# A two-layer attention and gated-product kernel: its orders, PSUM banks and strip places written out, up to six product steps inside a value burst

## The chip, the cores and the metric

The kernel runs on one core of one Trainium2 chip. The metric is the device time of one execution in microseconds (us); lower is better.

## The reference

Four stages run over one sequence of 2048 tokens of width 448. Stages 0 and 2 are the attention `A`, stages 1 and 3 the gated product `B`; each adds its result to `x`. The same weights serve both rounds.

```
x = A_x
x = x + A(layernorm(x), wqkv, wo)        # stage 0
x = x + B(layernorm(x), w_gate, w_up, w_down)   # stage 1
x = x + A(layernorm(x), wqkv, wo)        # stage 2
x = x + B(layernorm(x), w_gate, w_up, w_down)   # stage 3

A: q, k, v = x @ wqkv, 16 heads of 28; each token attends to itself and to the
   7 tokens 2, 4, ... 14 places before it; softmax; weighted sum of v; @ wo
B: (x @ w_gate) * (x @ w_up) @ w_down, inner width 1792
```

## The kernel before

**Tiles and stages.** Every stage is cut into chunks of 256 or 512 tokens (`ACH`, `BCH`), and the chunks of the four stages follow each other interleaved (`SEQ`), so that attention work of one round lies beside gate and up products of the next stage. `build` describes the whole kernel as some 1576 operations. Each one (`Op`) is a short run of instructions on one engine, with the operations it depends on and the PSUM banks it takes (`acquire`) and gives back (`release`). An operation is known by its number, which is the order in which `build` adds it and is the same in both kernels.

**What TensorE does.** There are four kinds of operations on it.
- Ordinary products (line L489): queries and keys (`xnTa,WQK`), values (`WV,xnTa`), the output projection (`wo_g,oT`), gate and up (`xnTb,WGU`), down (`WD,hT`). They are made of *steps*: a step is two instructions, one on the upper and one on the lower 64 rows of the array, which run side by side.
- Score bursts (L964): 64 small products of `qk`, for two blocks of 120 tokens.
- Value bursts (L1001): 64 small products (64 columns each) of `E_sb` and `v_sb`, again for two blocks; the first burst of a stage has 32. There are nine in each attention stage.
- Strips (L492): an ordinary step can also be written as eight instructions of 32 output columns each. In this form it uses the array in the same tiling as a value burst and can stand *inside* the burst. The operation whose steps are used so is called the host; what is left of it follows the burst in the ordinary form.

**What sets the order.** `ORD` lists, for each engine, the numbers of its operations in the order in which they are to run. An entry `526+393` on TensorE is burst 526 with host 393. `schedule` walks through these lists with a model of the times (`run_pe`, `ready_at`, the constants at the head of `Sched`). It uses the model to pick PSUM banks (`pick_banks`: the one free longest) and to decide in what order releases are seen. For an entry with a host it lays up to two steps (`MAXALT`, `WEAVE`) evenly into the burst: for 64 small products after the 21st and the 42nd. `emit` then writes the instructions of each engine in that order and puts the semaphore waits in front of an operation.

**Queues.** SyncE issues nearly all transfers, in one queue in the order of `ORD["sp"]`; an issue that waits for a semaphore holds up all behind it. At the start these are the tokens (`x_sb`), the four pieces of `wqkv` for queries and keys (`hT` is their staging place; two pieces go through ScalarE's queue), `WV`, `wo_g`, and then the 14 pieces of `WGU`. Each of the latter waits for the landing of the third transfer before it (`link`, `DEPTH`). Before the first product of queries and keys, eight casts (L664) bring the staged pieces into `WQK`; the first such product needs the halves of all four pieces.

Of the kernel before, what the change touches and what calls it, by code (L numbers as in the profile page):

```python
# [25 lines left out]
MAIN = "R64"  # L26
BURST = "C32"
WEAVE = 2
MAXALT = 2
# [18 lines left out]
NBK = 8  # L48
# [9 lines left out]
ORD = {  # L58
# [5 lines left out]
}  # L64
SEQ = "A00 A01 B10 A02 B11 A03 A04 B12 A20 B13 A21 B14 B30 A22 B31 A23 B32 B33 B34".split()

# [57 lines left out]
class Sched:  # L124
    ENGS = ("pe", "act", "dve", "pool", "sp")
    PE_LAT = 205.0
    LAT = 75.0
# [1110 lines left out]
```

## Time and profile before

| what | value |
|---|---|
| median of 3 runs | 387.16 us (386.94 to 387.19) |
| profiled execution: span from first to last instruction | 384.9 us |
| TensorE matrix products busy | 379.2 us, 6340 instructions |
| VectorE busy | 280.7 us |
| ScalarE busy | 194.2 us |
| GpSimd busy | 10.3 us |

The page gives the profiled execution as its span; the run times are about 2.3 us longer, and this lies outside the first and last instruction. In a timeline, a row starts at the given time and merges instructions of one form that follow each other; since products overlap in the array, a row's length reaches beyond the start of the next. The time a piece takes on the path is therefore read from start to start. In a table by stretch, (x32) after a busy time counts the instructions that are under way in that stretch.

### The profile page before, as it was taken

The numbers are of one execution on the slowest core, as the hardware profiler recorded it, in microseconds if no ns is written. First come the engines' busy times: TensorE is split into PE (matmuls) and PEld (weight loads), VectorE is DVE, ScalarE is ACT, GpSimd is POOL, SyncE is SP. The second block draws the span as 40 slices with busy tenths as digits, with TensorE's granted clock in tenths as the row PEclk, the third lists the DMA queues.
The fourth block names the chain that finished last, engine by engine and source line by source line (L and its number), as shares of the span: only waits on it lengthen the run. The fifth ranks groups of instructions, "written<-read, shape, count | busy, mean of one in ns | idle before, by whom it ended". The sixth has DMA issues, their size and how long they took to land.

```text
span 384.9 us, 14276 instructions
## 1 busy us (share of the span) xinstructions
PE 379.2 (99%) x6340; PEld 212.9 (55%) x6340; DVE 280.7 (73%) x605; ACT 194.2 (50%) x384; POOL 10.3 (3%) x41
## 2 busy tenths in 40 slices
PE   8999999999999999999999999999999999999997
PEld 4556577555554444444566677544555544445664
DVE  6977989889878678487887887764877796455333
ACT  5987885744753653154273535455365353134220
POOL 7110000000000000000000000000000000000000
PEclk9999999999999999999999999999999999999999
DMA  8887332501410012214003117120135014013003
GB/s 275 200 188 192 91 79 54 76 2 32 93 28 14 17 34 52 55 27 63 12 3 73 33 20 100 27 43 9 21 41 75 3 24 85 2 33 52 3 4 131
DMA packets 55105, 22.76 MB, mean 59 GB/s; under 512 B 46132, under 2 KB 54148, under 8 KB 55044
## 3 DMA queue, kind: packets, MB, share of 16 engines
q1 hardware_dynamic: 54612, 21.34, 27.1%
q8 instruction: 50, 0.82, 0.9%
q10 hardware_dynamic: 432, 0.52, 0.4%
q14 instruction: 11, 0.09, 0.1%
HBM read 8.54 MB, written 2.71 MB: 29 GB/s over the span
## 4 chain that ended last, share of the span: by engine, by line
PE 94%; DVE 3%; ACT 2%; issue 0%; DVEq 0%
PE ps L489 84%; PE ps L964 3%; PE ps L1001 2%; PE ps L655 2%; PE ps L1107 1%; PE ps L492 1%; ACT qk L852 1%; DVE xn_sb L748 1%; DVE O_sb L1012 1%; ACT E_sb L971 1%; PE ps L758 0%; DVE R_sb L1026 0%; DVE oT L1039 0%; DVE x_sb L1056 0%; ACT R_sb L1027 0%
## 5 line engine op out<-in xcount | busy, mean ns | idle before, releaser
L489 PE MATMUL ps<-xnTb,WGU 64*128 64x512 bf16 (+1 forms) x1938 | 176.7, 333 | 0.0
L489 PEld LDWEIGHTS ps<-xnTb,WGU 64*128 64x128 bf16 x1938 | 95.2, 94 | 71.1 <-issue 1.2
L1092 ACT ACTIVATE g_sb<-ps 128x512 bf16<-128x512 f32 (+1 forms) x140 | 69.5, 511 | 111.9 <-PE ps L489 105.3
L1095 DVE TENSOR_TENSOR hT<-g_sb,ps 128x512 bf16<-128x512 bf16 (+1 forms) x140 | 77.9, 574 | 37.9 <-ACT g_sb L1092 35.0
L489 PE MATMUL ps<-WD,hT 64*128 64x448 bf16 x820 | 84.4, 349 | 0.1
L489 PEld LDWEIGHTS ps<-WD,hT 64*128 64x128 bf16 x820 | 39.0, 94 | 34.5 <-issue 0.4
L1056 DVE TENSOR_TENSOR x_sb<-x_sb,ps 128x448 bf16<-128x448 bf16 x62 | 36.8, 614 | 23.5 <-PE ps L489 23.5
L489 PE MATMUL ps<-xnTa,WQK 64*128 64x512 bf16 (+1 forms) x504 | 52.1, 353 | 0.1
L727 DVE BATCH_NORM_STATS2 st<-x_sb 128x6 f32<-128x448 bf16 x64 | 38.3, 615 | 1.9 <-DMA x_sb<-in_A_x_dram 1.5
L748 DVE TENSOR_SCALAR xn_sb<-x_sb,mv,rstd 128x896 bf16<-128x896 bf16 (+1 forms) x64 | 35.5, 569 | 5.2 <-ACT rstd L732 5.1
L971 ACT ACTIVATE E_sb<-ps 128x1024 bf16<-128x1024 f32 (+1 forms) x36 | 33.8, 983 | 10.4 <-PE ps L964 9.7
L489 PEld LDWEIGHTS ps<-xnTa,WQK 64*128 64x128 bf16 x504 | 24.1, 94 | 22.7 <-POOL v_sb L628 0.5
L981 DVE TENSOR_TENSOR E_sb<-E_sb,MK 128x1024 bf16<-128x1024 bf16 (+2 forms) x40 | 23.5, 610 | 12.7 <-ACT E_sb L971 12.5
L852 ACT ACTIVATE qk<-ps 128x1024 bf16<-128x1024 f32 (+1 forms) x26 | 23.2, 907 | 14.4 <-PE ps L489 14.2
L489 PE MATMUL ps<-wo_g,oT 64*128 64x448 bf16 x252 | 28.7, 350 | 0.4 <-DVE oT L1039 0.2
L1039 DVE TENSOR_TENSOR oT<-O_sb,R_sb 128x480 bf16<-128x480 f32 (+3 forms) x36 | 22.0, 624 | 3.2 <-ACT R_sb L1028 3.2
L1027 ACT ACTIVATE R_sb<-R_sb 128x480 f32<-128x480 f32 (+1 forms) x34 | 20.1, 604 | 7.2 <-DVE R_sb L1026 6.9
L1026 DVE STREAM_SHUFFLE R_sb<-O_sb 128x480 f32<-128x480 f32 (+1 forms) x34 | 22.8, 694 | 0.0
L489 PE MATMUL ps<-WV,xnTa 64*128 64x336 bf16 (+3 forms) x244 | 22.6, 304 | 0.1
L730 ACT ACTIVATE lnv<-mv,eps_sb 128x2 f32<-128x2 f32 (+1 forms) x33 | 9.4, 293 | 26.4 <-DVE mv L729 26.4
L1028 ACT ACTIVATE R_sb<-R_sb 128x480 f32<-128x480 f32 (+1 forms) x34 | 19.7, 599 | 0.2
L489 PEld LDWEIGHTS ps<-wo_g,oT 64*128 64x128 bf16 x252 | 11.9, 94 | 11.5 <-PE ps L489 1.0
(55 smaller groups left out, 190.6 us busy)
## 6 DMA issues: line engine op xcount, KB each, us to landing
out_dram<-x_sb SPq DMA_DIRECT2D x15, 112.0 KB, 1.8
WGU<-in_B_w_gate_dram SPq DMA_DIRECT2D x7, 224.0 KB, 4.3
WGU<-in_B_w_up_dram SPq DMA_DIRECT2D x7, 224.0 KB, 4.2
x_sb<-in_A_x_dram SPq DMA_DIRECT2D x3, 448.0 KB, 5.8
WD<-in_B_w_down_dram SPq DMA_DIRECT2D x2, 448.0 KB, 3.6
WD<-in_B_w_down_dram SPq DMA_DIRECT2D x2, 336.0 KB, 4.5
vt<-qk SPq DMA_DIRECT2D x42, 16.0 KB
xnTb<-xn_sb SPq DMA_TRANSPOSE x32, 3.1
```

Of the source, the lines that this page charges most:

```text
L489: return lambda E: E.matmul(out(), lhs(), rhs(), start=start, stop=stop)
L727: sc.add("dve", one(lambda E, B=B: E.bn_stats(st6[:, B, :], x_sb[:, B, :]), ("bn", li, B)), 525.0, deps=[("x", li - 1, B)] + ([("xn", li - ...
L748: sc.add("dve", one(lambda E, B=B, dst=dst, src=src: E.tensor_scalar(dst, src, mv[:, B, 0:1], rstd[:, B:B + 1], ALU.subtract, ALU.mult), ( ...
L852: return E.activation(dst, src, ACT.Copy) if hasattr(E, "activation") else E.tensor_copy(dst, src)
L971: return E.activation(E_sb[:, slot, 2 * hp:2 * hp + 2, 0:w], ps[:, b0:b0 + 2, 0:w], ACT.Exp, scale=SCALE)
L981: return E.tensor_tensor(e, e, m, ALU.mult)
L1026: sc.add("dve", one(lambda E: E.stream_shuffle(R_sb[:, rs, 0:w], O_sb[:, os_, 0:w], [DH] * 32), ("Rs", li, qb)), dve_est(w) + 100.0, deps= ...
L1027: sc.add("act", one(lambda E: E.activation(R_sb[:, rs, 0:w], R_sb[:, rs, 0:w], ACT.Ln), ("Rl", li, qb)), act_est(w, False), deps=[("Rs", l ...
L1039: return E.tensor_tensor(oT[:, :, a % HALF:a % HALF + z - a], O[:, :, a - tok:z - tok], R_sb[:, rs, 0:w].rearrange("p (h n) -> p h n", h=4 ...
L1056: sc.add("dve", one(lambda E: E.tensor_tensor(x_sb[:, B, :], x_sb[:, B, :], ps[:, bk[w], 0:D], ALU.add), ("x", li, B)), dve_est(D), deps=[ ...
L1092: sc.add("act", one(lambda E, gs=gs, bk=bk: E.activation(g_sb[:, gs, 0:nt], ps[:, bk[0], 0:nt], ACT.Copy), ("G", li, j, fc)), act_est(nt), ...
L1095: sc.add("dve", one(lambda E, gs=gs, bk=bk, fc=fc: E.tensor_tensor(hT[:, fc, hs, 0:nt], g_sb[:, gs, 0:nt], ps[:, bk[1], 0:nt], ALU.mult), ...
```

## The change

Three things change together.

1. **Orders.** All five lists of `ORD` are new. No operation is added or removed. Some 40 evacuations and casts go to another engine; among them the three casts (L664) that ScalarE had go to GpSimd, which now does all eight. In SyncE's queue the first transfers are reordered, and four of the `WGU` pieces now stand behind writes of `vt` (columns of the values of late query chunks).
2. **Banks.** `schedule` no longer holds a model of the times. It reads the banks of each operation from a new list `BANK`, walks the lists once, and adds the waits for the former holder of a bank.
3. **Strip places.** `MAXALT` is 6, and an entry with a host gives the places of its steps: `253+349@24.40` lays one step after the 24th and one after the 40th small product. A number that occurs twice means two steps at that place. There are 14 entries with a host in both kernels. Before, they hold 27 steps, afterwards 46, that is 19 more steps in strips. TensorE has 6454 products instead of 6340.

The core of the diff, the lists cut to the entries with hosts and to the heads of two queues:

```
-WEAVE = 2
-MAXALT = 2
+MAXALT = 6
...
 "pe", entries with a host:
-526+393 402+583 547+444 597+587 618+660 761+684 774+681
-918+846 939+852 1127+1009 1148+1187 1301+1226 1322+1235 1343+1237
+253+349@24.40 526+393@24.32.40 547+444@16.16.32.40 597+482@24.40
+618+560@24.40 761+684@8.24 774+678@24.40 918+846@8.24.32.40.48
+939+855@24.40 1127+1009@8.23.32.32.40 1148+1193@24.32.40.40
+1301+1235@8.16.24.40.48.48 1322+1227@16.24.40.48 1343+1313@24.32.48
...
 "sp", first entries (0 1 6 7 8 11: x_sb; 4 5: staged pieces 1 and 3; 9 10: WV):
-0 1 4 5 6 7 8 9 10 11 12 13
+0 4 1 6 7 5 8 81 9 10 11 79 82 84 83 12 13
...
 "pool", first entries (62 to 69: the eight casts):
-18 43 23 20 24 27 19 34 63 62 28 64 68 69
+18 23 31 27 43 19 38 34 32 24 39 20 62 63 66 67 64 68 25 69 65
...
+BANK = "44:01 110:67 114:23 130:67 ... "
...
     def schedule(self):
+        banks = {}
+        for x in BANK.split():
+            i, got = x.split(":")
+            banks[int(i)] = [int(c) for c in got]
...
+            op.acquire.b = banks[op.idx]
+            for i, b in enumerate(op.acquire.b):
+                if holder[b] is not None:
+                    rel = freed[holder[b]]
+                    key = ("rel", rel.idx, b)
+                    self.ready[key] = (rel, len(rel.ins) - 1)
+                    op.deps.append(key)
+                holder[b] = (id(op.acquire), i)
...
-                            cut = [len(op.ins) * (i + 1) // (k + 1) for i in range(k)] + [len(op.ins)]
+                    cut = [int(c) for c in cuts.split(".")]
+                    seq, a = [], 0
+                    for i, z in enumerate(cut + [len(burst.ins)]):
+                        seq += [(burst, n) for n in range(a, z)]
+                        a = z
+                        if i < len(cut):
+                            seq += [(host, fn) for fn in host.alt[i]]
+                    seq += [(host, n) for n in range(2 * len(cut), len(host.ins))]
```

More of the change, by code (lines that the diff above doesn't have):

```diff
@@ L58 @@
 ORD = {
[5 rows of a table removed]
[5 rows of a table added]
 }
+BANK = "44:01 110:67 114:23 130:67 133:23 136:01 139:23 154:23 157:01 160:45 163:01 178:01 181:67 184:23 187:01 199:67 201:23 203:01 205:45 211:45 215:2345 220:23 228:67 230:23 232:01 234:45 240:67 244:23 248:0167 253:45 265:45 269:6701 274:67 286:45 300:67 303:01 306:05 309:41 312:06 315:23 318:47 321:15 324:64 327:75 330:17 333:60 336:26 339:16 342:54 348:67 350:23 352:23 354:45 367:67 371:67 376:6745 381:23 393:45 397:0123 402:23 414:67 438:03 441:23 444:26 447:01 450:21 453:67 456:52 459:67 462:72 465:34 468:16 471:05 474:10 477:34 480:32 486:67 492:45 494:01 496:23 498:01 511:45 516:67 521:0123 526:23 538:34 542:2301 547:45 559:01 563:45 565:01 567:45 569:01 582:01 587:67 592:6745 597:45 609:45 613:0167 618:45 630:01 654:13 657:32 660:04 663:15 666:67 669:40 672:23 675:67 678:12 681:45 684:23 687:60 690:17 693:23 696:62 702:34 728:23 730:45 732:01 734:67 747:23 751:01 756:6723 761:45 769:0167 774:45 786:46 810:76 813:15 816:20 819:17 822:26 825:67 828:23 831:12 834:40 837:75 840:46 843:45 846:75 849:64 852:35 858:16 884:23 886:01 888:45 890:67 903:23 908:01 913:2301 918:23 930:74 934:0167 939:67 951:23 965:40 968:70 971:72 974:42 977:31 980:10 983:35 986:32 989:54 992:72 995:53 998:63 1001:75 1004:24 1007:67 1023:53 1026:43 1029:67 1032:01 1035:43 1038:52 1041:01 1044:01 1047:67 1050:23 1053:23 1056:32 1059:50 1062:24 1065:46 1093:01 1095:67 1097:45 1099:01 1112:67 1117:01 1122:6745 1127:23 1139:23 1143:4501 1148:01 1160:23 1184:53 1187:30 1190:24 1193:72 1196:75 1199:01 1202:17 1205:34 1208:67 1211:45 1214:51 1217:20 1220:67 1223:46 1226:45 1234:32 1262:01 1264:45 1266:67 1268:01 1281:45 1286:01 1291:01 1296:2367 1301:67 1313:13 1317:4501 1322:01 1334:07 1338:6701 1343:45 1355:76 1379:36 1382:24 1385:27 1388:72 1391:05 1394:41 1397:36 1400:13 1403:52 1406:75 1409:41 1412:60 1415:07 1418:63 1421:20 1429:14 1457:53 1460:65 1463:41 1466:03 1469:57 1472:02 1475:02 1478:56 1481:41 1484:57 1487:20 1490:35 1493:05 1496:73 1499:62 1507:45 1525:17 1528:34 1531:16 1534:12 1537:37 1540:63 1543:01 1546:63 1549:01 1552:41 1555:60 1558:71 1561:01 1564:72 1567:7 1570:6 1573:3"
 SEQ = "A00 A01 B10 A02 B11 A03 A04 B12 A20 B13 A21 B14 B30 A22 B31 A23 B32 B33 B34".split()
@@ L108 @@
     __slots__ = ("engs", "ins", "est", "deps", "mode", "prio", "acquire", "release", "idx", "eng",
-                 "dma", "lat", "after", "start", "end", "seen", "selfd", "tmin", "rdy", "alt", "pos")
+                 "dma", "lat", "after", "seen", "selfd", "tmin", "alt")
     def __init__(self, **kw):
@@ L125 @@
     ENGS = ("pe", "act", "dve", "pool", "sp")
-    PE_LAT = 205.0
-    LAT = 75.0
-    SAME = 60.0
-    SELF_LAT = 180.0
-    TAIL = {"pe": 0.0, "act": 125.0, "dve": 85.0, "pool": 100.0, "sp": 0.0}
-    SWITCH = 102.0
-    FETCH = 4.17
-    QUEUE = 64
-    AHEAD = 32
-    HEAD = 64
-    REFILL = 256.0
-    LINE = 256
-    LINE_T = ((75000.0, 4300.0), (24000.0, 4900.0), (11000.0, 5600.0), (-1.0, 5000.0))
     def __init__(self):
@@ L142, in __init__ @@
         self.ready = {}
-        self.fed = [(self.HEAD, 0.0)]
-        self.lines = [0.0, 0.0]
-        self.npos = 0
-        self.met = {}
     def add(self, engs, ins, est, deps=(), prio=0.0, mode=None, acquire=None, release=(), dma=None, lat=0.0, after=None, selfd=(), tmin=None, alt=()):
@@ L162, in add @@
         return op
-    def finish_of(self, key):
-        op, n = self.ready[key]
-        if op.end is None:
-            return None
-        if op.dma is not None:
-            return max(o.end + o.lat for o in self.dgroup[(op.dma, op.mode)])
-        if n == len(op.ins) - 1:
-            return op.end
-        return op.start + (op.end - op.start) * (n + 1) / len(op.ins)
-    def ready_at(self, op, eng):
-        r = 0.0
-        for k in op.deps:
-            f = self.finish_of(k)
-            if f is None:
-                return None
-            src = self.ready[k][0]
-            if src.dma is not None:
-                lat = 60.0
-            elif src.eng == eng:
-                lat = (self.SELF_LAT if k in op.selfd else 0.0) if eng == "pe" else self.SAME + self.TAIL[eng]
-            else:
-                lat = self.PE_LAT if src.eng == "pe" else self.LAT + self.TAIL[src.eng]
-            r = max(r, f + lat)
-        if op.tmin is not None:
-            r = max(r, op.tmin)
-        if op.after is not None:
-            if op.after.end is None:
-                return None
-            r = max(r, op.after.end)
-        return r
@@ L196, in pick_banks @@
-    def pick_banks(self, req, now):
-        ok = [self.holder[b] is None and self.free_at[b] + self.LAT <= now + 1e-6 for b in range(NBK)]
-        if req.pair:
-            pairs = [p for p in range(NBK // 2) if ok[2 * p] and ok[2 * p + 1]]
-            if len(pairs) < req.n // 2:
-                return None
-            pairs.sort(key=lambda p: max(self.free_at[2 * p], self.free_at[2 * p + 1]))
-            got = []
-            for p in pairs[:req.n // 2]:
-                got += [2 * p, 2 * p + 1]
-            return got
-        cand = [b for b in range(NBK) if ok[b]]
-        if len(cand) < req.n:
-            return None
-        cand.sort(key=lambda b: (ok[b ^ 1], self.free_at[b]))
-        return cand[:req.n]
@@ L213, in banks_for @@
-    def banks_for(self, item, now):
-        held, ok = list(self.holder), True
-        for op in item:
-            if op.acquire is not None:
-                got = self.pick_banks(op.acquire, now)
-                if got is None:
-                    ok = False
-                    break
-                for b in got:
-                    self.holder[b] = op.acquire
-        self.holder = held
-        return ok
-    def fed_at(self, i, ahead):
-        i = max(0, i - ahead)
-        for (n0, t0), (n1, t1) in zip(self.fed[-2::-1], self.fed[:0:-1]):
-            if n0 <= i:
-                return t0 + (t1 - t0) * (i - n0) / max(1, n1 - n0)
-        return 0.0
@@ L235, in run_pe @@
-    def run_pe(self, now, n, stream):
-        n0 = self.fed[-1][0]
-        t = now
-        if self.fed[-1][1] < now:
-            self.fed.append((n0, now))
-        lead = min(self.QUEUE, (now - self.fed_at(n0, self.QUEUE)) / self.FETCH)
-        end = now + stream
-        if n > lead:
-            end = max(end, now + (n - lead) * self.FETCH + self.REFILL)
-        while len(self.lines) * self.LINE <= n0 + n + self.AHEAD:
-            k = len(self.lines)
-            i = (k - 1) * self.LINE
-            if i <= n0:
-                at = self.fed_at(i, self.AHEAD)
-            else:
-                at = max(now, now + (end - now) * (i - n0 - self.AHEAD) / n)
-            at = max(at, self.lines[-1])
-            self.lines.append(at + next(t for t0, t in self.LINE_T if at >= t0))
-        k = (n0 + n) // self.LINE
-        if k * self.LINE > n0:
-            due = now + (end - now) * (k * self.LINE - n0) / n
-            end += max(0.0, self.lines[k] - due)
-        self.fed.append((n0 + n, end))
-        del self.fed[:-48]
-        return end
@@ L262, in waits @@
-    def waits(self, got):
-        need = {}
-        for op in got:
-            for k in op.deps:
-                src, n = self.ready[k]
-                if src.dma is not None:
-                    need[(src.dma, src.mode)] = (1, 0)
-                elif src.eng != "pe" or k in op.selfd:
-                    need[src.eng] = max(need.get(src.eng, (0, 0)), (src.pos, n))
-        new = 0
-        for w, v in need.items():
-            if self.met.get(w, (0, 0)) < v:
-                self.met[w] = v
-                new += 1
-        return max(0, new - 1)
@@ new lines, in schedule, with take @@
+    def schedule(self):
+        banks = {}
+        for x in BANK.split():
+            i, got = x.split(":")
+            banks[int(i)] = [int(c) for c in got]
+        freed = {}
+        for op in self.ops:
+            for bk, i in op.release:
+                freed[(id(bk), i)] = op
+        order = {e: [] for e in self.ENGS}
+        holder = [None] * NBK
+        seen = set()
+        def take(op, e):
+            assert op.idx not in seen and e in op.engs, (op.idx, e)
+            seen.add(op.idx)
+            op.eng = e
+            if op.acquire is None:
+                return
+            op.acquire.b = banks[op.idx]
+            assert len(op.acquire.b) == op.acquire.n and not (op.acquire.pair and any(x ^ 1 not in op.acquire.b for x in op.acquire.b))
+            for i, b in enumerate(op.acquire.b):
[5 more added lines that the diff above has]
+                holder[b] = (id(op.acquire), i)
+        for e in self.ENGS:
+            for x in ORD[e].split():
+                ids, _, cuts = x.partition("@")
+                got = [self.ops[int(i)] for i in ids.split("+")]
+                for op in got:
+                    take(op, e)
+                seq = [(got[0], n) for n in range(len(got[0].ins))]
+                if len(got) > 1:
+                    burst, host = got
+                    cut = [int(c) for c in cuts.split(".")]
[6 more added lines that the diff above has]
+                    seq += [(host, n) for n in range(2 * len(cut), len(host.ins))]
+                order[e].append((got, seq))
+        assert len(seen) == len(self.ops)
@@ L408, in schedule @@
         self.order = order
-        self.total = max(op.end + op.lat for op in self.ops)
     def emit(self, nc, block, sems):
```

123 lines of the change are left out of this document (removed), and 10 rows, old and new, of the table ORD.

## The prediction

> **What bounds the kernel now.** I read the page's head first, then the chain that ended last, then the busy times by stretch, then timelines of TensorE where it was not plain streaming.
>
> ```profile
> span 384.9 us, 14276 instructions
> ...
> PE 379.2 (99%) x6340; PEld 212.9 (55%) x6340; DVE 280.7 (73%) x605; ACT 194.2 (50%) x384; POOL 10.3 (3%) x41
> ...
> PE 94%; DVE 3%; ACT 2%; issue 0%; DVEq 0%
> ```
>
> TensorE (PE) carries 94% of the chain that sets the end. The stretches tell where it does not:
>
> ```profile
> core 0: us, PE busy (x) PEld busy (x) DVE busy (x) ACT busy (x) POOL busy (x), PEclk, DMA share, GB/s
> 8.00:22.00 14.00, 13.27 (x301) 8.23 (x296) 13.26 (x43) 13.15 (x33) 4.38 (x20) 1.00 0.83 222
> 22.00:36.00 14.00, 13.77 (x286) 8.26 (x269) 11.30 (x26) 12.26 (x24) 0.12 (x1) 1.00 0.80 180
> 36.00:52.00 16.00, 15.59 (x440) 8.14 (x438) 13.30 (x28) 13.47 (x21) 0.00 (x0) 1.00 0.51 125
> 52.00:66.00 14.00, 13.94 (x356) 11.99 (x357) 13.26 (x31) 9.43 (x22) 0.00 (x0) 1.00 0.16 34
> 66.00:130.00 64.00, 63.71 (x1127) 34.08 (x1124) 50.97 (x113) 37.15 (x69) 0.00 (x0) 1.00 0.24 41
> 130.00:258.00 128.00, 127.94 (x2122) 72.80 (x2118) 99.63 (x210) 57.05 (x119) 0.00 (x0) 1.00 0.24 42
> ```
>
> From 8 to 52 us (the head) TensorE is idle for 0.73 + 0.23 + 0.41 = 1.37 us, and VectorE and ScalarE are nearly as full as it is (13.26 and 13.15 of 14 us at first). From 52 to 130 us it is idle for 0.35 us, and from there to 258 us for 0.06 us. The granted clock is 1.00 throughout. So better orders can win at most about 1.4 us in the head and 0.35 us behind it; after 130 us they can only lose. What else is to be had lies inside TensorE's busy time, in the value bursts.
>
> **The bursts.** Timelines of TensorE: a burst without a host, one with a host, and ten gate-and-up operations without a burst.
>
> ```profile
> 27.23 0.68 PE L1001 MATMUL ps<-E_sb,v_sb 64*32 64x64 bf16 x64
> 27.85 0.74 PE L489 MATMUL ps<-WV,xnTa 64*128 64x448 bf16 x6
> ...
> 141.64 0.27 PE L1001 MATMUL ps<-E_sb,v_sb 64*32 64x64 bf16 x21
> 141.73 0.40 PE L492 MATMUL ps<-xnTb,WGU 64*32 64x512 bf16 x8
> 141.96 0.26 PE L1001 MATMUL ps<-E_sb,v_sb 64*32 64x64 bf16 x21
> 142.04 0.52 PE L492 MATMUL ps<-xnTb,WGU 64*32 64x512 bf16 x8
> 142.26 0.39 PE L1001 MATMUL ps<-E_sb,v_sb 64*32 64x64 bf16 x22
> 142.58 1.90 PE L489 MATMUL ps<-xnTb,WGU 64*128 64x512 bf16 x16
> ...
> 307.04 15.27 PE L489 MATMUL ps<-xnTb,WGU 64*128 64x512 bf16 x140
> 322.14 0.92 PE L489 MATMUL ps<-wo_g,oT 64*128 64x448 bf16 x8
> ```
>
> An ordinary step of 512 columns costs (322.14 - 307.04) / 70 = 0.216 us. A burst alone costs 27.85 - 27.23 = 0.62 us. The woven one takes 142.58 - 141.64 = 0.94 us and does two steps on the way, so the burst itself costs 0.94 - 0.43 = 0.51 us. The laying-in is worth 0.11 us a burst as it stands. Why a burst alone is so slow shows when it is cut finer:
>
> ```profile
> 27.23:27.35 0.12, 0.12 (x32) 1.00 1.26 286
> 27.35:27.45 0.10, 0.10 (x32) 1.00 1.37 198
> 27.45:27.72 0.27, 0.27 (x58) 1.00 0.08 2
> ```
>
> The first 32 products enter within 0.12 us. Then for 0.10 us the same 32 are under way and none enters; the other 32 then need 0.27 us. I read this as a window of 32 products: product n + 32 enters when product n has left. The Trainium skill ("TensorE: Matmul & The Clock Gate", section "Architectural detail: the array is 16× 32×32, not 1× 128×128") gives TensorE a queue of 64 instructions; a weight load and a matmul for each product make 32 products, and the trace agrees (x32). By its rule that matmuls also end in order (same page, "The mechanism"), a strip that is still running keeps everything behind it in the window.
>
> If the window never bound, 64 products would enter in 2 x 0.12 = 0.24 us, and the way out (27.72 to 27.85) is 0.13 us: 0.37 us. So a burst that is woven already can gain between 0 and 0.51 - 0.37 = 0.14 us. In the woven burst above, the first set of strips lasts 0.40 us and the second 0.52 us: the second enters one by one, because with the cut at 21 and 42 its strips are the 51st to 58th products, and from the 54th on they wait for the first set (the 22nd to 29th) to leave. With the cut at 24 and 40, 24 products and 8 strips fill the window exactly, and the next 16 products and the second strips (33rd to 56th) wait only for the first 24 small products, which leave long before the first strips end. The second set then lasts 0.40 us again: a gain of 0.12 us, of which I take 0.10.
>
> Sum over the bursts: 13 entries woven before and after, one of them half as long, 12.5 x 0.10 = 1.25 us. Burst 253 is newly woven: 0.62 - 0.41 = 0.21 us. Burst 402 loses its host: 0.11 us lost. That makes -1.35 us, with bounds of 0 (no cut helps; 253 and 402 cancel) and -1.9 us (0.14 each, 253 at 0.25). The 19 further steps are work that is moved, not removed. Inside the burst a step takes 141.96 - 141.73 = 0.23 us instead of 0.216 us, so they cost between 0 and 19 x 0.014 = 0.27 us; I take 0.1. That a third to sixth step hides anything more I don't count: with two well-placed ones the burst is already near 0.4 us.
>
> **The start.** The first query and key product needs the casts of all four staged pieces.
>
> ```profile
> 1.71 0.91 SPq L579 DMA_DIRECT2D hT<-in_A_wqkv_dram  x2
> 2.66 1.50 SPq L579 DMA_DIRECT2D x_sb<-in_A_x_dram  x3
> ...
> 6.37 1.07 POOL L664 COPY WQK<-hT 128x448 bf16<-128x448 bf16 x2 [0.25 <-DMA hT<-in_A_wqkv_dram]
> ...
> 7.43 1.04 ACT L664 ACTIVATE WQK<-hT 128x448 bf16<-128x448 bf16 x2
> 7.64 0.39 PE L489 MATMUL ps<-xnTa,WQK 64*128 64x256 bf16 x4
> ...
> x_sb<-in_A_x_dram SPq DMA_DIRECT2D x3, 448.0 KB, 5.8
> ```
>
> The last staged piece, issued at about 2.2 us (the second of the two in the first row), lands just ahead of 6.37 us, 4.1 us later. In the new queue two token transfers (224 and 448 KB) stand in front of it, and it is issued two places, 0.9 us, later, at 3.1 us. If it takes 4.1 us again, it lands at 7.2 us; if it takes the 5.8 us of the big token transfers, at 8.9 us. I take 8.2, nearer to the latter, since those tokens now go first. With a cast of 0.53 us the product can start at about 8.8 instead of 7.64 us: 1.2 us late, with bounds of 0.1 and 1.8. The Trainium skill ("DMA: Bandwidth & Descriptors", "Queues, rings and completion order") says that each engine takes a queue's descriptors in ring order; by that rule the upper part of the range is right, without it the lower.
>
> This start need not reach the end. The tokens land earlier by what the piece lost, VectorE begins sooner, and ScalarE, which has no idle time to speak of, is rid of three casts (3 x 0.52 = 1.6 us), which GpSimd does in time it has. The first gate product ends the head:
>
> ```profile
> 50.01 1.93 PE L489 MATMUL ps<-wo_g,oT 64*128 64x448 bf16 x16 [0.24 <-DVE oT L1039]
> 51.92 0.83 PE L489 MATMUL ps<-xnTb,WGU 64*128 64x256 bf16 x12
> ```
>
> TensorE has 51.92 - 7.64 - 1.37 = 42.9 us of work up to there. From 8.8 us on without any idle time it would arrive at 51.7, 0.2 us sooner; with all the idle time left, 1.2 us later. The idle time was waiting for the engines that are now relieved, so I take +0.1 us.
>
> **The rest.** Of the 0.35 us between 52 and 130 us I take 0.1 as won. Behind it, some fifteen evacuations change between ScalarE and VectorE; TensorE hid them all (0.06 us idle in 128), VectorE has 28 us to spare there, and I cost them at nothing. If a few banks come free late, each costs what is left of an evacuation, up to 0.5 us in all.
>
> **Sum.** -1.35 + 0.1 + 0.1 - 0.1 = -1.25 us. The span of 384.9 becomes 383.6. The runs' median is 2.3 us above the span, which I leave unchanged: 387.16 - 1.25 = 385.9 us.
>
> **Rivals.** *The head opens up:* the late start is absorbed in full and the waits between 52 and 130 us go too, with the bursts at their bound: -1.9 - 0.2 - 0.35 = -2.45, 384.7 us. For it speaks that ScalarE is relieved; against it that TensorE's start is later.
>
> *The window is not what holds the bursts:* if the entry rate of 0.27 us for 32 products is set by something that strips use up too, the new cuts give nothing, the 19 steps cost 0.27 us, and with the head at +0.1: 387.5 us; with half of the gain 386.8. Against it: the first set of strips enters at full rate.
>
> *SyncE's queue makes the first gate product late, so the kernel is slower:* four of the 14 gate and up pieces now stand behind writes of `vt`, which wait for evacuations of late query chunks, and two of the four wait for the landing of the other two. Timeline of SyncE's queue, and the table of issues:
>
> ```profile
> 9.97 0.57 SPq L579 DMA_DIRECT2D WGU<-in_B_w_gate_dram  x1
> ...
> 17.43 0.47 SPq L579 DMA_DIRECT2D WGU<-in_B_w_up_dram  x1
> ...
> 44.63 1.71 SPq L751 DMA_TRANSPOSE xnTb<-xn_sb  x1
> ...
> WGU<-in_B_w_up_dram SPq DMA_DIRECT2D x7, 224.0 KB, 4.2
> ```
>
> The last piece now stands between the two transposes for the first gate product, so it is issued at 44.63 + 1.71 = 46.3 us and lands, at the median of 4.2 us, at 50.5: 1.4 us ahead of 51.92. But a piece can take longer: the fourth was issued at 17.43 us because it waits for the first, which had been issued at 9.97, 7.5 us before. At 7.5 us the last piece lands at 53.8, the product is 1.9 us late, and with the piece that it waits for late as well (3.3 us more, of which I guess half is covered) 3.5 us: 387.16 + 3.5 - 1.35 = 389.3 us. It decides from a landing at 51.9 us on. Against it: the transfers are only 0.51 busy from 36 to 52 us, against 0.83 when the first piece took so long.
>
> **Chances.** About 0.2% (0.77 us) is what can be told from no change here. My forecast with its own range of 385.2 to 386.8: 0.50; the open head 0.17; the window reading wrong 0.15; the late gate product 0.18. Faster by over 0.2% (under 386.4): 0.38 of the first and the open head, 0.55. Within: 0.12 of the first and most of the third, 0.25. Slower: the late product and a rest, 0.20. The range leaves out the far ends of the open head and of the late product: 384.3 to 388.6.
>
> **What would show it.** In the new trace: bursts with two steps at 24 and 40 cost about 0.41 us beyond their steps (right) or 0.5 (wrong); the second strips row lasts 0.40 us; the first row of `xnTa,WQK` starts at 8.3 to 9.3 us; the first gate product at 51.5 to 52.5 us; no new waits of TensorE behind 130 us. The prediction is wrong if the first gate product comes after 53 us, or if bursts with four to six steps cost less than 0.3 us each beyond their steps.

## The result and the profile after

The changed kernel is 1.1% slower, well clear of the noise; the forecast was 385.9 us, with a range up to 388.6.

| kernel | median us (runs) | ratio to before, 95% interval | span of the profiled execution |
|---|---|---|---|
| before | 387.11 (386.94 to 387.19) | | 384.9 us |
| after | 391.19 (390.36 to 392.06) | 1.0108, 1.0090 to 1.0125 | 389.7 us |

The medians below are over all runs of a kernel; a ratio goes to the runs of before that were taken beside it, disturbed runs left out, so the two can differ by a tenth of a per cent.

The head of the new page, the lines that answer to the first three of the prediction:

```profile
span 389.7 us, 14474 instructions
...
PE 378.4 (97%) x6454; PEld 214.8 (55%) x6454; DVE 274.7 (70%) x603; ACT 195.0 (50%) x384; POOL 11.4 (3%) x43
...
PE 94%; DMA 2%; DVE 2%; issue 1%; ACT 0%; SPq 0%
```

TensorE is busy for 0.8 us less, with more products, in a span that is 4.8 us longer. It is idle for 11.3 us instead of 5.7. In the chain, "issue" has grown from 0% to 1%: time in which an engine waited for nothing that the profile shows. The chain in order of time (start, duration, what) tells where:

```profile
43.46 0.45 PE ps L787 x44
43.91 0.56 issue
44.47 0.27 PE ps L787 x20
...
48.07 1.67 PE ps L275 x21
49.74 1.44 issue
51.18 0.73 PE ps L275 x7
...
289.32 0.02 PE ps L787 x5
289.34 1.59 issue
290.93 0.24 PE ps L787 x11
```

Three stops, 0.56 + 1.44 + 1.59 = 3.59 us, each in the middle of an operation: in burst 274, in the value product 372, in burst 1301. An operation's semaphores are waited for ahead of its first product, so neither a semaphore nor a bank can be the reason. In the chain of before, no "issue" stands at these places (its one long one, 0.62 us at 62.59, lies between two operations of VectorE, and the kernels with b_ have it too).

The second stop costs more than its length. Windows around it (length, busy times, then granted clock, DMA share, GB/s), and timelines of TensorE behind it:

```profile
50.00:51.00 1.00, 0.00 (x0) 0.00 (x0) 1.00 (x4) 0.79 (x2) 0.00 (x0) 1.00 0.50 106
53.00:54.00 1.00, 0.95 (x6) 0.15 (x2) 0.00 (x0) 1.00 (x2) 0.00 (x0) 0.50 0.22 47
```

```profile
9.32 0.94 PE L275 MATMUL ps<-xnTa,WQK 64*128 64x256 bf16 x14 [0.23 <-ACT lnv L516]
...
52.48 3.21 PE L275 MATMUL ps<-wo_g,oT 64*128 64x448 bf16 x16
55.48 0.82 PE L275 MATMUL ps<-xnTb,WGU 64*128 64x256 bf16 x6
...
66.83 0.28 PE L787 MATMUL ps<-E_sb,v_sb 64*32 64x64 bf16 x24 [0.90 <-ACT g_sb L878]
```

After a window with no product at all, the granted clock is 0.50. By the trace's clock record it stays there from 52.73 to 56.14 us, 3.41 us, which costs half of that, 1.7 us. The 16 products of `wo_g` take 3.21 us where before they took 1.93. The first gate product therefore starts at 55.48, far behind the 53 us from which the prediction called itself wrong. The last row is another loss: burst 526 waits 0.90 us. The row names an activation, but a_wgu and after_again name other operations at the same wait, and in all of them and in a_shift48 the burst starts 0.24 to 0.25 us after the value transposes that it needs have landed (here at 66.58). So it waits for these.

The bill of the span, +4.8 us: the first product 1.7 us late (9.32 against 7.64), stops 3.6, half clock 1.7, burst 526 0.9, a gate product that waits for its transpose 0.3 (at 117.1), together 8.2. Against it stand the bursts, about -1.5 (read from start to start, less their steps and stops), and -1.9 that is left over. Of that, 1.0 us is idle time that the new orders took out: from the first product to 130 us it was 1.7 us, and is 0.7 us now beside the stops and waits of this bill. What made up the rest, shorter busy time, is open.

### The profile page after: what moved, and what is told of

Read it like the earlier page. It is cut to its first block, busy times and chain, and to the rows that moved or that the text cites. A ratio compares the mean times of both kernels' runs of the same rounds, so it can differ in the third digit from the quotient of the medians.

```text
span 389.7 us, 14474 instructions
## 1 busy us (share of the span) xinstructions
PE 378.4 (97%) x6454; PEld 214.8 (55%) x6454; DVE 274.7 (70%) x603; ACT 195.0 (50%) x384; POOL 11.4 (3%) x43
## 4 chain that ended last, share of the span: by engine, by line
PE 94%; DMA 2%; DVE 2%; issue 1%; ACT 0%; SPq 0%
PE ps L275 85%; PE ps L750 3%; PE ps L278 2%; PE ps L787 2%; PE ps L893 1%; DMA xnTb<-xn_sb 1%; DMA x_sb<-in_A_x_dram 1%; DVE st L513 0%; PE ps L544 0%; DVE O_sb L798 0%; DVE E_sb L767 0%; DVE xn_sb L534 0%; SPq L365 0%; DVE xnTa L552 0%; ACT lnv L516 0%
## 5 line engine op out<-in xcount | busy, mean ns | idle before, releaser
L275 PE MATMUL ps<-xnTb,WGU 64*128 64x512 bf16 (+1 forms) x1926 | 174.6, 333 | 0.3 <-DMA xnTb<-xn_sb 0.3
L275 PE MATMUL ps<-WD,hT 64*128 64x448 bf16 x802 | 83.0, 349 | 0.0
L275 PEld LDWEIGHTS ps<-WD,hT 64*128 64x128 bf16 x802 | 40.3, 94 | 32.0 <-DVE v_sb L730 0.2
L534 DVE TENSOR_SCALAR xn_sb<-x_sb,mv,rstd 128x512 bf16<-128x512 bf16 (+1 forms) x64 | 36.1, 580 | 2.0 <-ACT rstd L518 2.0
L275 PEld LDWEIGHTS ps<-xnTa,WQK 64*128 64x128 bf16 x500 | 23.2, 94 | 22.8 <-ACT E_sb L757 0.9
L638 ACT ACTIVATE qk<-ps 128x1024 bf16<-128x1024 f32 (+1 forms) x28 | 25.9, 949 | 16.1 <-PE ps L275 16.0
L798 DVE COPY O_sb<-ps 128x448 f32<-128x448 f32 (+2 forms) x22 | 13.5, 637 | 9.6 <-PE ps L787 9.3
```

The source lines that it names most:

```text
L275: return lambda E: E.matmul(out(), lhs(), rhs(), start=start, stop=stop)
L534: sc.add("dve", one(lambda E, B=B, dst=dst, src=src: E.tensor_scalar(dst, src, mv[:, B, 0:1], rstd[:, B:B + 1], ALU.subtract, ALU.mult), ( ...
L638: return E.activation(dst, src, ACT.Copy) if hasattr(E, "activation") else E.tensor_copy(dst, src)
```

## What the stops are

TensorE's instructions are loaded by a queue of their own. The profile's table of queues has it:

```profile
q8 instruction: 51, 0.84, 0.9%
```

These are 51 packets of 16 KB for the 13,055 instructions of TensorE that the trace has, so a packet is a *line* of 256 instructions. The trace records each packet. Beside the three stops (instructions counted from 0 at the start of the trace, those that only wait for a semaphore included):

```
stop in after       packet started  took   ended    TensorE goes on   later by   instruction
burst 274             41.88         1.12    43.01      44.46            1.45        1729
product 372           48.57         1.18    49.75      51.18            1.43        1985
burst 1301           288.50         0.99   289.49     290.93            1.44       10433
```

TensorE goes on 1.43 to 1.45 us after the end of a packet, and the first instruction that it then runs is always number 193 + 256 k (k = 6, 7, 40). So each stop is the end of a line whose successor is not there yet. At none of the 99 line ends of the two profiles that have a packet does TensorE pass more than 0.1 us before the end of that packet + 1.43 us. The Trainium skill ("Runtime: NRT & Kernel Launch", section "Instruction fetch mechanics") says that the sequencer fetches blocks of 256 instructions through a DMA queue of its own while it works on the one before. The trace agrees. The page also calls the cost of crossing a block mostly hidden; here it is 3.6 us of stops in one execution, and the measurement decides.

A value or a score burst is 128 instructions in some 0.6 us, an ordinary step 4 instructions in 0.2 us. The line that ends in burst 1301 holds a score burst and most of a value burst with its steps, and is used up in 2.5 us. A step laid into a burst is 16 instructions instead of 4: the 19 further steps are 228 more instructions, which sit in the densest lines and also move every later line end.

*Theory:* the loss is late lines, and the clock that falls behind them. *Rivals:* the waits come from the new orders, banks and engines; the bursts with four to six steps hold TensorE up; SyncE's queue delays weights.

In the experiments, labels with b_ are the kernel before with edits, those with a_ the changed kernel with edits.

## Experiments

**b_c24: the strip places alone**

```
-cut = [len(op.ins) * (i + 1) // (k + 1) for i in range(k)] + [len(op.ins)]
+cut = ([24, 40] if k == 2 else [16]) + [len(op.ins)]
```

> The kernel before with one edit: in the 13 value bursts of 64 products that already carry two steps, the steps stand after the 24th and the 40th product instead of the 21st and 42nd. Same orders, banks and number of instructions. Theory (the window term of the prediction is right, and the loss of the changed kernel lies elsewhere): each of these bursts costs 0.42 us beyond its steps instead of 0.51, together -1.2 us: 385.9 us, ratio 0.997. Rival (the cheaper bursts that the new trace shows come from the new orders, not from the places): 387.1 us, ratio 1.000.

Measured: 386.18 us, ratio 0.9978 (0.9968 to 0.9988). The burst that the prediction quoted at 141.64, in the new timeline its first row, the second set of strips and the row behind it:

```profile
141.51 0.28 PE L1001 MATMUL ps<-E_sb,v_sb 64*32 64x64 bf16 x24
...
141.88 0.40 PE L492 MATMUL ps<-xnTb,WGU 64*32 64x512 bf16 x5
...
141.91 0.40 PE L492 MATMUL ps<-xnTb,WGU 64*32 64x512 bf16 x3
...
142.33 1.04 PE L489 MATMUL ps<-xnTb,WGU 64*128 64x512 bf16 x8
```

From 0.94 to 0.82 us: 0.39 beyond its steps instead of 0.51. The second set of strips lasts 0.40 us, as the window reading said, instead of 0.52. Summed over the 13 bursts it is 1.16 us: 0.116 us each with a host of 512 columns, 0.088 with 448, 0.01 to 0.04 with 336. 0.3 us of it were lost again to a gate product that waited for its transpose. The sum of the burst term was right; that a burst gains less with a narrower host is not in it.

**b_shift192 and a_shift48: the same work, other line ends**

```
+parts = (0, 104, 208, 312, 416, 512) if n < 12 else (0, 512)   # b_shift192; n < 3: a_shift48
-  one product of columns 0:512 for each half of warm-up operation n
+  one product for each pair of neighbours in parts
```

> The kernel before with its first 12 warm-up operations written as five narrower products each in place of one: the same columns, 96 products and so 192 TensorE instructions more, in a stretch in which TensorE waits for the first casts. Everything behind is the same, but each instruction stands 192 places later in the program. Theory (TensorE's instructions are loaded in lines of 256, and a line that is used up in less than some 2.7 to 4.1 us makes TensorE wait for the next): counted on the trace of before, the lines that then end near 22.2 and 241.8 us last only 2.84 and 1.44 us, so there is a wait of 1.3 to 2.7 us near 242 us, perhaps one near 22 us, and the kernel takes 388.4 to 391 us. Rival (the waits of the changed kernel come from its orders and its banks): 387.1 us within 0.3.

Measured: 391.4 us, ratio 1.0121 (1.0086 to 1.0156), 0.4 us above the expected range. The chain has two stops that before does not have, at the two places foretold:

```profile
24.06 0.84 issue
244.33 0.76 issue
```

Both end at a line's end (instructions 961 and 9153). But they are 1.6 us of a span that is 4.1 us longer. The start is 0.8 us later, since the warm-up lasts longer, the first value product waits 1.2 us for `WV`, and the last output takes 0.8 us longer to land. Whether the last two belong to the shift these runs do not tell.

> The changed kernel with its first three warm-up operations written as five narrower products each: 24 products, 48 instructions more, ahead of a stretch in which TensorE waits anyway. Orders, banks and strip places are untouched. Theory (lines of 256 instructions that arrive late): the wait of 1.59 us inside burst 1301 near 290 us is gone, since the line that ends there now lasts over 4.2 us; new waits of some 0.5 to 1.5 us come near 104 us and 245 us, where lines then last 2.5 us; the whole within 1.5 us of the changed kernel's 391.2. Rival (the six steps of host 1235, or the semaphores ahead of 1301, hold it up): the wait near 290 us stays at 1.6 us and none comes near 104 and 245 us.

Measured: 391.51 us, ratio 1.0117 (1.0076 to 1.0159). The stop in burst 1301 is gone with its six steps untouched (0.38 us beyond them), and five new ones are there:

```profile
49.72 0.77 issue
...
107.28 0.19 issue
112.53 0.63 issue
144.05 0.58 issue
249.67 0.72 issue
```

Two were expected, near 104 and 245 us; those at 113 and 144 us were not, but their line ends fit as well (4545 and 5569, as 4289 and 9153). The first, inside a score burst, is no line's end: TensorE goes on at instruction 2143, and what held it stays open. It is the only one of its kind. Of the 35 stops of over 0.1 us in the fourteen profiles that no wait stands in front of, 34 end at a line's end, 1.2 to 1.6 us behind the end of a packet. For the stop in burst 1301, the rivals "six steps" and "semaphores" fall. This profile also shows what burst 526 waits for:

```profile
65.93 0.29 PE L792 MATMUL ps<-E_sb,v_sb 64*32 64x64 bf16 x24 [3.09 <-DMA v_sb<-vt]
```

The value transposes stand in SyncE's queue behind writes of `vt`, the ones and a down piece; here they came 3.1 us late, and the clock stood at 0.50 from 67.16 to 70.58 us, behind this wait.

**a_wgu: four weight pieces back in front**

```
 "sp":
-87 88 577 578 98 366 91 362 90 364 576 580 94 299 93 297
+87 88 91 90 94 93 577 578 98 366 362 364 576 580 299 297
```

> The changed kernel with four weight pieces (91, 90, 94, 93) back ahead of the first writes of vt in SyncE's queue, so that none stands between the two transposes for the first gate product. TensorE's list is untouched. Theory A (the line that stops product 372 near 50 us is late because the transfers that run beside it hold up its loading): the wait of 1.44 us near 50 us shrinks to under 0.3, the granted clock stays at 1.00 behind it, the first gate product starts at about 52.3 us instead of 55.5, and the time falls by 2.5 to 3.5 us to about 388.2. Theory B (the line is late because TensorE uses up instructions too fast there, whatever is transferred): no change, 391.2 within 0.5. Rival (the first gate product waits for the last weight piece, as the prediction's third rival has it): the wait of 0.33 us just ahead of that product goes, 390.9.

Measured: 390.41 us, ratio 1.0092 (1.0078 to 1.0106). Near 50 us theory A holds:

```profile
49.91 0.71 PE L750 MATMUL ps<-qk 28*64 28x64 bf16 x64
50.55 1.93 PE L275 MATMUL ps<-wo_g,oT 64*128 64x448 bf16 x16
52.46 0.72 PE L275 MATMUL ps<-xnTb,WGU 64*128 64x256 bf16 x10
```

No stop, the clock at 1.00, the gate product 3.0 us sooner. The line is used up in 5.0 us in both kernels. Its packet started 4.1 us after TensorE had entered the line before in after, 3.0 us here, and in dense stretches without transfers mostly 0.7 to 1.2 us. So what the queue moves beside it seems to make a line late, too; the 1.1 us rest on one edit, and most of the delay is still there. The end gained only 0.8 us of the 2.5 to 3.5 expected: burst 526 now waits 1.5 us (0.9 in after) and the stop in burst 1301 lasts 1.86 us.

**a_fix and a_fixhead: the other waits, and the start**

```
 a_fix = a_wgu and
 "sp": the ones (96) ahead of 299; 97 99 100 behind 515 514 374 375
-"pe": 1234 1317 1301+1235@8.16.24.40.48.48 1291 1226 1292 1236
+"pe": 1234 1317 1235 1301+1291@24.40 1226 1292 1236
 a_fixhead = a_fix and
-"sp": 0 4 1 6 7 5 8 81 9 10 11 79 82 84 83 12 13 78
+"sp": 0 1 4 5 6 7 8 9 10 11 12 13 81 79 82 84 83 78
```

> The changed kernel with three edits: the four weight pieces early, as in a_wgu; the write of the ones and three down pieces (96; 97, 99, 100) no longer among the last writes of vt and the transposes 515, 514, 374, 375 behind them; and burst 1301 moved behind host 1235, which now runs as ordinary products, with 1291 laid into the burst instead. Theory (the loss is late instruction lines, plus the value transposes that wait for those writes): the wait ahead of burst 526 (0.68 us in the changed kernel, 1.28 in a_wgu) is under 0.2; near 288 us the line gets one operation of 1.5 us more, with fewer small products, and the wait of 1.59 to 1.86 us there falls to about 0.6; the rest as in a_wgu, 390.4 - 1.2 - 1.1 = 388.1 us. Rival (the new orders of ScalarE and VectorE behind 130 us cost the time): 390.4 within 0.4.

Measured: 388.81 us, ratio 1.0052 (1.0028 to 1.0077). The stop near 288 us falls to 0.47 us and the wait of burst 526 goes. But my edit made a wait of its own, since the last down piece now comes late:

```profile
69.88 0.55 PE L275 MATMUL ps<-WD,hT 64*128 64x448 bf16 x4 [1.68 <-DMA WD<-in_B_w_down_dram]
```

> a_fix with SyncE's first twelve transfers as before: all tokens and staged pieces in the old order, so that the second staged piece stands fourth again. It tests the prediction's step that the late start (9.3 instead of 7.6 us) is absorbed by 52 us. If it is absorbed: the first query and key product starts at 8.0 to 8.5 us, the first gate product still at 52.3 to 52.6, and the time is that of a_fix within 0.3. If not: both come 0.7 to 1.2 us sooner, and so does the end.

Measured: 388.27 us, ratio 1.0025 (1.0005 to 1.0046). The start moves from 9.08 to 8.17 us and the first gate product from 53.55 to 52.01:

```profile
8.17 1.05 PE L275 MATMUL ps<-xnTa,WQK 64*128 64x256 bf16 x16
...
52.01 1.25 PE L275 MATMUL ps<-xnTb,WGU 64*128 64x256 bf16 x19
```

0.5 us of the 1.5 are shorter stops (0.43 and 0.34 instead of 0.69 and 0.62); the rest is the earlier start, which was not absorbed by then. The end came 0.5 us sooner by the medians; the two intervals overlap, so that this reaches the end is likely but not shown.

**b_weave1 and b_weave3: one host more, and three**

```
 both: b_c24's places, and the banks of before written out
 b_weave1   -178 349 253 244      +178 253+349@24.40 244
 b_weave3   as b_weave1, and
            -274 493              +274+493@24.40
            -381 372              +381+372@24.40
```

> The kernel before with the strip places of b_c24 (24 and 40) and one more host, 349 laid into burst 253; orders otherwise and banks as in before. Bursts: 0.21 us less. The two more steps in strips are 24 instructions more from 29 us on. Theory of the lines: counted on the trace of b_c24, with 24 more every line lasts over 3.9 us, so no wait appears: 386.0 us, ratio 0.997 or a little below, and the profile has no wait of TensorE over 0.3 us that ends 1.3 to 1.6 us after a line was loaded. If instruction lines don't matter: the same, 386.0.

Measured: 385.57 us, ratio 0.9963 (0.9945 to 0.9980), the fastest kernel of the study and 0.4 us below what was expected. Its chain has no stop that before does not have.

> As b_weave1, with two hosts more: 493 laid into burst 274 and 372 into burst 381, so that all but one of the bursts of 64 ahead of 60 us carry steps. Bursts: three times 0.21 us less than b_c24. The six steps in strips are 72 instructions more from 47 us on. Theory of the lines: counted on the trace of b_c24, with 72 more the lines that end near 102 and 285 us last only 2.6 us, and the one near 47 us 3.2 us; at 0.3 to 1.5 us for each that is late, 386.0 to 388.5 us, with the waits at just these places. If instruction lines don't matter: 385.6 us, and no waits there.

Measured: 388.36 us, ratio 1.0031 (1.0015 to 1.0046): two more hosts, which should have saved 0.4 us, make the kernel slower. The chain's "issue" rows that b_weave1 lacks:

```profile
46.22 0.26 issue
...
52.00 0.72 issue
...
103.34 0.49 issue
286.76 0.68 issue
```

They end at instructions 1985, 2241, 4289 and 10433. Three are at the places foretold; that at 52 us was not expected.

**b_weave3_s208 and b_weave1_s48: the lines of these two exchanged**

```
 b_weave3_s208  parts = (0, 104, 208, 312, 416, 512) if n < 13 else (0, 160)
 b_weave1_s48   parts = (0, 104, 208, 312, 416, 512) if n < 3 else (0, 512)
```

> b_weave3 with nothing else changed than its warm-up: the first 13 of the 18 warm-up operations are written as five narrower products each (104 products, 208 instructions more that compute nothing), the last five are shortened from 512 to 160 columns, to make up for the time. Theory of the lines: counted on the trace of b_weave3, with 208 more the lines that were late near 46, 53, 104 and 287 us now last 3.7 to 4.5 us, the shortest (3.4 us) ends near 22 us; so the waits of 0.26, 0.71, 0.49 and 0.68 us go, and the time falls from 388.36 by 1.5 to 2.8 us to 385.5 to 386.9 (the lower end if no new wait comes near 22 us). Rival (the three hosts themselves, or waits for semaphores, cost what b_weave3 lost): 388.4 us or more, since there are more instructions.

Measured: 387.8 us, ratio 1.0010 (0.9988 to 1.0033), between what the theory and the rival gave; the time alone does not decide. All four stops are gone. The line near 22 us is late instead (0.92 us), and the first value product waits for `WV` again:

```profile
12.78 0.65 PE L275 MATMUL ps<-WV,xnTa 64*128 64x224 bf16 x8 [1.43 <-DMA WV<-in_A_wqkv_dram]
```

From burst 381 on, this kernel takes 335.1 us to its last product, b_weave3 338.1, with the same products.

> b_weave1 with one edit: the first three warm-up operations are written as five narrower products each, 24 products or 48 instructions more at the start, nothing else. Orders, banks, hosts and strip places are those of b_weave1. Theory of the lines: counted on the trace of b_weave1, where every line lasts 4 us or more, with 48 more the lines that end near 47, 102 and 285 us last 3.2, 2.6 and 2.6 us; b_weave3, whose lines stood at the same places, waited 0.3, 0.5 and 0.7 us there. So waits of TensorE appear near 102 and 285 us (and perhaps 47), of 1.2 to 2 us together, and the start is up to 0.3 us later: 386.8 to 387.8 us. Rival (what b_weave3 lost came from its two further hosts): 385.6 to 385.9 us.

Measured: 388.19 us, ratio 1.0040 (1.0021 to 1.0059). The start is no later (7.54 us), hosts and banks are those of the fastest kernel, and 24 more products at the start, which compute nothing that is used, cost it 2.6 us, 0.4 more than the top of the expected range. Stops:

```profile
14.71 0.31 issue
...
102.84 0.19 issue
...
139.66 0.37 issue
286.57 0.35 issue
```

They end at 449, 4289, 5569 and 10433. Two are where they were foretold, the one near 47 us did not come, and those at 15 and 140 us were not on the list. In the profiled execution the stops are 1.2 of the 1.8 us by which its span is longer (385.7 against 383.9); where the rest comes from is open.

**after_again**

> The changed kernel once more, for a second profile. If its waits are late lines, they come at the same instructions again: inside bursts 274 and 1301 and product 372, of about 0.5, 1.6 and 1.4 us, though their lengths may differ with the transfers that run beside; the wait ahead of burst 526 varies. Time 390.4 to 392.1 us.

Measured: 390.73 us, ratio 1.0093 (1.0066 to 1.0119), span 389.7 us.

```profile
43.81 0.43 issue
49.52 1.17 issue
...
287.29 1.59 issue
298.88 0.32 issue
```

The same three instructions, and one more line that was just in time in the first profile. The half clock follows another stop now: it runs from 289.19 to 292.60 us, behind the 1.59 us. Without it near 50 us, and with a stop there that is 0.3 us shorter, the first gate product comes at 53.89 instead of 55.48 us.

**a_best**

```
 a_fixhead and
 "sp": 97 ahead of 96 299; 99 100 right behind 515 514
+parts = (0, 104, 208, 312, 416, 512) if n < 1 else (0, 512)
```

> a_fixhead with two edits: the three down pieces that a_fix put behind the value transposes stand earlier (97 ahead of the first transposes for the gate products; 99 and 100 right behind 515 and 514), since the wait of 1.65 us near 68 us is a down product waiting for the last of them; and one warm-up operation written as five narrower products, 16 instructions more. Theory: the wait near 68 us is under 0.2; of the line waits of 0.43, 0.34 and 0.76 us near 43, 49 and 288 us half goes, since these lines last up to 0.4 us longer: 388.27 - 1.5 - 0.7 = 386.1 us, ratio 0.998. Rival (a wait removed comes back elsewhere, as it did at 68 us): 387.5 us or more.

Measured: 386.34 us, ratio 0.9972 (0.9957 to 0.9987). Of the stops inside an operation one of over 0.15 us is left, at a line's end (instruction 10945):

```profile
293.73 0.35 issue
```

With nearly all of its orders and burst places, the changed kernel becomes 0.3% faster than before once SyncE's queue and the line ends are put right. The kernel before with the strip places and one more host (b_weave1, ratio 0.9963) does as well, so no gain of the new orders and banks themselves shows.

## Why the prediction was wrong

- **The bursts: right.** -1.25 us was forecast for the places in 12.5 bursts; b_c24 gives 1.16 us in 13. In after, burst 253 takes 0.39 us beyond its two steps and those with four and five steps 0.36 to 0.40, as "near 0.4" said. The rival that the window does not hold the bursts is refuted: b_c24 is outside of 387.1.
- **The extra steps and their loading: the step that failed.** "Work that is moved, not removed", 0 to 0.27 us: as products they cost nothing measurable. They were not priced as instructions. The prediction had no term for loading instructions at all, though `run_pe`, which the diff takes out, keeps an account in lines of 256 (`LINE`, `LINE_T`). The missing term is 3.6 us of stops and 1.7 us of half clock, more than the whole loss of 4.1 us. It has two parts. The stops in bursts 274 and 1301 (2.15 us) end lines used up in 3.4 and 2.5 us, where the lines that end at the same instruction numbers in before lasted 4.0 and 4.7 us: more and denser instructions. The stop in product 372 (1.44 us), with the half clock behind it, ends a line of 5.0 us, as in before (5.1), whose packet started 4.1 us late instead of 1.0; here SyncE's new queue is the likelier reason (a_wgu). b_weave1_s48 shows that late lines cost time without any change of the work.
- **"After 130 us nothing", "no new waits of TensorE behind 130 us": wrong** by the stop of 1.59 us in burst 1301. The moved evacuations, which it was argued for, did cost nothing: this stop is all the idle time of TensorE from 130 us to its last product.
- **The start: right in time and reason.** The last staged piece was issued at 3.17 us and landed at 8.65, its cast ended at 9.26, and the product came at 9.32, within the bounds around 8.8. That the late start "need not reach the end" held less well: in a_fixhead the old start moves the first gate product as well.
- **The head, +0.1: nearly right.** In a_wgu the first gate product comes at 52.46 us (forecast 51.5 to 52.5), 0.5 us later than before, and 0.4 of it is the stop in burst 274. The start, 1.3 us late there, is paid in full. What is gained back is 0.6 us of other idle time, where the sum had counted on 1.1, and 0.6 us of shorter busy time, of which the prediction had 0.2 (burst 253) among the bursts. That the total came so near is in part luck.
- **From 52 to 130 us, -0.1:** instead +0.9 us for burst 526, whose value transposes stand too late in SyncE's queue.
- **The rival of SyncE's queue (389.3 us)** had the right sign and came nearest in size, but by another way. The last weight piece was issued at 45.86, took 4.8 us and had landed by 50.7, ahead of 51.9, its point of decision. The queue did matter: for burst 526, and most likely for the line at 50 us.

The gate product's lateness, which the prediction named as the sign of being wrong, was the right place to look; only the chain's word "issue" told that no wait of the program was behind it.

## What to carry to other kernels

Before you make TensorE's instructions smaller and more, count them: where 256 follow each other in less than about 4 us, ask when the next 256 arrive. In these runs all ten lines used up in under 2.7 us made TensorE stop, 15 of the 38 from 2.7 to 4 us, and 9 of some 650 longer ones, all but one of these (0.11 us) beside transfers at a DMA share of 0.5 and more. When a wait stands as "issue" inside an operation, shift the program by some cheap instructions and profile again: a late line's stop moves to other operations, a wait for a semaphore stays with its own.

## What the hardware showed

- Where a line was late, TensorE went on 1.2 to 1.6 us after its packet had ended, and a packet took 0.9 to 2.0 us.
- Where a line ends can be worth microseconds: 48 instructions at the start moved the same kernel by 2.6 us (385.57 to 388.19), of the size of the change's whole loss (4.1 us).
- Behind a stop of 1.4 to 1.6 us the granted clock stood at 0.50 for 3.41 us (after, after_again), and so it did behind a wait of 3.1 us (a_shift48); but a stop of 1.86 us in a_wgu did not, nor did the 1.59 us in the first profile of after. The Trainium skill ("TensorE: Matmul & The Clock Gate", section "🔬 Part 1: The HAM clock gate (the "warmup" mystery)") has the clock fall after an idle window of about 3.4 us. The length of the half clock agrees; the stops ahead of it here are shorter than that, and why only some of them are followed by it stays open.
- Also open: why the packet of a late line starts up to 4.1 us after TensorE has entered the line before. a_wgu points to the transfers beside it, and so do the three late lines that were not foretold at 113 us (a_shift48), 52 us (b_weave3) and 15 us (b_weave1_s48): their packets started 3.4 to 3.9 us after that, at a DMA share of 0.71, 0.65 and 1.13 over that time. Which transfers, and by what, was not tried. They are not the only reason: in a_best a packet started 5.5 us after TensorE had entered the line before (316.48 and 311.02 us), at a DMA share of 0.01; that line lasted 12.9 us, so it cost nothing.
